# Attention into a mixture of experts: key maxima, one-hots, halves of w1 and four clears dealt anew to the attention's steps

## The chip, the core and the metric

The kernel runs on one core of one Trainium2 chip. A core has engines that each work through their own instructions in order: TensorE (PE in the rows) multiplies matrices into PSUM; VectorE (DVE), ScalarE (ACT) and GpSimd (POOL) work on elements; SyncE (SP) issues DMA transfers. They wait for each other through semaphores. The metric is the device time of one execution in microseconds, lower is better. Times before are the median of three runs.

## What is computed

First attention over 4 batches, 8 heads, 768 positions of width 64, with keys of a local window of 16 to either side and with one summary key and value for every block of 32 positions (the maximum of the block's keys, the mean of its values). The result, 3072 rows of 512 numbers, goes through a mixture of 8 experts, of which each row uses the two with the largest noisy gate:

```python
k_sum = k.reshape(B, H, nb, block, D).max(axis=3)
v_sum = v.reshape(B, H, nb, block, D).mean(axis=3)
...
a = np.exp(scores_all)
a = a / (np.sum(a, axis=-1, keepdims=True) + 1e-09)
...
top2 = np.argpartition(-noisy_logits, 2, axis=1)[:, :2]
...
h = np.maximum(x[mask] @ w1[e], 0.0)
out[mask] += top2_w[mask, k, None] * (h @ w2[e])
```

`out` starts as zeros. In the kernel that is done by eight DMA writes of zeros ("clears"), 384 rows or 768 KB each, after which the experts add their rows by gather and scatter.

## The kernel before

The attention works on 24 tiles of 128 rows, six to a batch. A loop over steps t is software-pipelined: in step t TensorE makes the scores of tile t + 2 (`mask_sums`, L316, and `scores`, L326), multiplies tile t's weights with its values (`av`, L365), transposes tile t + 1's weights (`p_trans`, L348) and tile t - 1's result (`x_pe`, L419). VectorE takes the row maxima of the scores (`smax`, L336 and L337: `nm`, which ScalarE's exponentials L342 need) and normalizes tile t (`norm`, L396 to L400). GpSimd lays out the keys of tile t + 3 (`kx`, L126, L131) and splits the result into two halves of float16 (L406, L411), which SyncE stores to `xd` (`x_out`, L414). SyncE also loads the queries four steps ahead (`load_q`, L118) and the values two steps ahead (`v_load`, L296 and L297). Step 9 begins on TensorE at 56.38 us, step 10 at 62.59, step 11 at 70.53, step 13 at 78.01, step 16 at 95.81, step 17 at 100.95, step 18 at 105.74 and step 21 at 118.42.

Everything else in the attention is hung into the steps by a table: `at(time, f, ...)` puts a call at a step number with a fraction, and the fraction says where in the step's code `run` or `vector_work` takes it. So t + 0.02 stands right behind the step's store of `x`, t + 0.1 behind VectorE's normalization of the step, t + 0.9 at its end. What hangs there and is touched by the change:

- `k_piece` (L232, tile `kmax`): the maxima over blocks of the keys of one pair of heads; four for each batch, in `KP`. `load_k` (L112, tile `kb`) loads the keys of two pairs of heads, at the times in `KL`. Batch b's keys lie in buffer b % 2.
- `gate_lh`, `gate_o`, `gate_f` (L592, L624, L631): for a group of four tiles, one-hots of a row's place (`lh`, `oc`) and their product with the row's values (`rh`); `gate_t` (L643) multiplies them on TensorE one step later, and `gate_u` (L647) adds that to the table `acc`, from which the experts' row numbers are decoded (`decode`, L654 to L660) in step 19. `make_table` holds the steps of a group.
- `w_load` (L716 for w1, L719 for w2; tile `stg`, four buffers), and `w_part`: the first expert's w1 comes in four pieces of 512 KB, each split in halves into a high float16 part (ScalarE, L737) and the rest (VectorE, L735, tile `w1l`). The four loads of w2 at 17.9, 18.9, 21.9 and 22.9 take the same four buffers, so each waits for the halves that read the piece before it.
- `x_gather` (L94) and `x_trans` (L862): in steps 20 and 21 GpSimd gathers three chunks of 128 of the first expert's rows from `xd`, and SyncE transposes them by DMA into `xte`. Right after the attention TensorE multiplies these with w1 (`mm1_pe`, L884).
- `clear` (L1101): one write of zeros to 384 rows of the output, from a tile of zeros. `XG[3]` is a gather buffer that is cleared at the very start and first gathered into after the attention.

After the attention the first expert's products begin with 384 columns, while the last tables are made; then come the other seven experts, in which TensorE is fed from prefetched weights and gathered rows.

Of the kernel before, what the change touches and what calls it, by code (L numbers as in the profile page):

```python
# [8 lines left out]
F32 = mybir.dt.float32  # L9
# [53 lines left out]
def attn_moe(ctx, tc, qt, kt, vt, wgn, noise, w1, w2, out):  # L63
# [150 lines left out]
    XG = []  # L214
# [198 lines left out]
    def x_out(t):  # L413
        xd_w.append(nc.sync.dma_start(xd[t * P:(t + 1) * P], XR[t]))  # L414
# [221 lines left out]
    def gate_t(b, o, hs=(0,), i=1):  # L636
        tb = o[:, i, GO:GO + 3 * NS]
        n = 2 * GN * len(hs)
        for h in hs:
            lh, rh, _ = GR[b, h]  # L640
            for j in range(2 * GN):
                n -= 1
                nc.tensor.matmul(tb, lh[:, j], rh[:, j], start=(h == hs[0] and j == 0), stop=(n == 0),  # L643
                                 skip_group_check=True)

    def gate_u(b, o, i=1):
        nc.vector.tensor_add(ACC, ACC, o[:, i, GO:GO + 3 * NS].rearrange("p (v c) -> p v c", v=3))  # L647
# [44 lines left out]
    def w_alloc(e):  # L692
        w1_alloc(e)
        w2_alloc(e)
# [398 lines left out]
    def at(t, f, *a):  # L1093
        todo.setdefault(round(t, 3), []).append((f, a))
# [3 lines left out]
    def clear(zero, n):  # L1098
        a = cleared[0]
        cleared[0] += n  # L1100
        nc.sync.dma_start(out[a * P:(a + n) * P].rearrange("(c p) d -> p c d", p=P),  # L1101
                          zero[:, None, :].to_broadcast([P, n, DM]))
# [15 lines left out]
    at(0.2, v_sums_out, 0)  # L1118

    w_alloc(0)  # L1120
    for i, (l, h, z) in enumerate(((6, 8, 9), (7, 9, 10), (15, 19, 20), (16, 20, 21))):
        at(l, w_load, 0, i)
        for k in range(2):
            at(h + 0.9, w_part, i, k, 0)
            at(z + 0.1, w_part, i, k, 1)
    VS = [4, 10, 15]
    KP = ((1, 1, 2, 2), (5, 6, 7, 8), (10, 12, 13, 14))
    KL = ((-1, 0), (3, 5), (9, 10))
    VL = [(1, 2), (6, 7), (12, 13)]
    for b in range(B - 1):  # L1130
        for h in range(HP):
            at(KP[b][h] + 0.1, k_piece, b + 1, h)
            if h % 2 == 0:
                at(KL[b][h // 2], load_k, b + 1, h, 2)
        for i in range(2):
# [6 lines left out]
    for i in range(3):  # L1142
        at(4.9 + 2 * i, fill, i)
    at(20.8, last_init)
    for g in range(5):
        u = 4 * g + 6
        at(u - 0.7, gate_gt, g)
        at(u - 0.65, gate_gc, g)
        at(u + 0.3, gate_gl, g)
        at(u + 0.35, gate_gd, g)  # L1150
# [22 lines left out]
    def make_table(b, v, lh, oc, rh):  # L1173
        at(v + 0.8, gate_v, b, False)
        at(lh + 0.1, gate_lh, b)
        at(oc + 0.1, gate_o, b)
        at(rh + 0.1, gate_f, b)
        at(rh + 1.28, lambda b, t: gate_t(b, PO[t], (0,)), b, rh + 1)
        at(rh + 1.4, lambda b, t: gate_u(b, PO[t]), b, rh + 1)

    make_table(0, 10, 11, 11, 13)
    make_table(1, 13, 14, 15, 15)
    make_table(2, 16, 17, 17, 18)
    at(19.1, decode, TB0, 0, 3)
    at(22.6, gate_a, 4)
    at(22.8, gate_v, 3, False)

# [24 lines left out]
    for t in range(-2, NT - 1):  # L1212
        u = t + 3
# [103 lines left out]
    gate_p(4)  # L1317
    spair.close()
    banks.append(ctx.enter_context(tc.tile_pool(name="banks", bufs=4, space=PSUM, reuse_waits="tile")))
    for i in range(4):  # L1320
        clear(PREV[2], 3)
    x_out(NT - 1)
    for i in range(4):
        clear(PREV[2], 3)
    w_load(1, 0, "sh0")
    w_load(1, 2, "sl0")
# [259 lines left out]
```

## Time and profile before

| | |
|---|---|
| median of three runs | 649.4 us (647.72 to 653.26) |
| profiled execution, its own time | 649.54 us |
| its span in the trace | 647.7 us |
| TensorE busy | 625.7 us, 97% of the span |
| VectorE busy | 478.5 us, 74% |
| GpSimd busy | 349.9 us, 54% |
| ScalarE busy | 306.3 us, 47% |

The span is the stretch between the first and the last recorded instruction; 1.8 us of the execution lie outside. A busy share says how long an engine worked, not whether others waited for it; for that one looks in the engine's order of time at the idle stretch before an instruction and at what released it. In the rows below, the time in brackets is that idle stretch.

### The profile page before, as it was taken

What the parts mean: (1) busy time and instruction counts of PE and PEld (TensorE: products, weight loads), DVE (VectorE), ACT (ScalarE), POOL (GpSimd) and SP (SyncE); (2) the same over time, 40 slices, a digit from 0 to 9 for tenths busy, and PEclk for the clock granted to TensorE, in tenths of its full rate; (3) what the DMA queues carried; (4) which work ended last, traced back from release to release, by engine and by line L of the source; (5) the groups of instructions that cost most, each with busy time, mean ns of one, the idle gap of its engine ahead of it and who ended that gap; (6) DMA issues with size and microseconds to landing.
All of it is one profiled execution on the core that took longest, in us unless ns stands there. A gap on an engine that the chain in (4) does not pass through costs nothing.

```text
span 647.7 us, 14116 instructions
## 1 busy us (share of the span) xinstructions
PE 625.7 (97%) x5407; PEld 368.3 (57%) x5407; DVE 478.5 (74%) x897; ACT 306.3 (47%) x647; POOL 349.9 (54%) x531
## 2 busy tenths in 40 slices
PE   8998899899999999999999999999999999999996
PEld 7777678765545544554465446545554555455543
DVE  7858898886786879577947886787778677956511
ACT  3788787851533552265235424541564165325300
POOL 5675777735635757653655465555546451632042
PEclk9999999999999999999999999999999999999999
DMA  8999998899978686456835572667266723431031
GB/s 302 321 331 376 300 356 280 197 339 312 274 162 181 212 181 184 157 194 159 210 134 167 164 237 102 196 162 232 97 182 160 236 72 110 149 127 50 2 100 52
DMA packets 104568, 125.63 MB, mean 194 GB/s; under 512 B 58393, under 2 KB 59681, under 8 KB 104492
## 3 DMA queue, kind: packets, MB, share of 16 engines
q1 hardware_dynamic: 92348, 88.37, 46.4%
q0 software_dynamic: 12144, 36.28, 17.9%
q8 instruction: 44, 0.72, 0.5%
q14 instruction: 32, 0.26, 0.1%
HBM read 87.38 MB, written 26.21 MB: 175 GB/s over the span
## 4 chain that ended last, share of the span: by engine, by line
PE 76%; issue 8%; DMA 6%; DVE 4%; POOL 2%; ACT 1%; POOLq 1%; SPq 0%; another core or an unknown queue 0%; ACTq 0%; DVEq 0%
PE pt L1039 33%; PE h L920 23%; DMA q<-in_qt_dram 5%; PE h L884 4%; PE a L920 4%; PE pt L1036 3%; PE o L365 2%; PE s L326 2%; PE pt L348 2%; DMA kb<-in_kt_dram 1%; POOL prev L94 1%; PE pt L419 1%; DVE s L336 1%; POOL out_dram L94 1%; PE pt L439 1%
## 5 line engine op out<-in xcount | busy, mean ns | idle before, releaser
L94 POOL DMA_INDIRECT out_dram<-y,tb x48 | 64.5, 1345 | 153.4 <-DVE y L1062 140.7
L1039 PEld LDWEIGHTS <-hth 128*128 128x128 f16 x768 | 74.9, 98 | 89.1
L1039 PE MATMUL pt<-w2h,htl 128*128 128x512 f16 x376 | 88.8, 379 | 0.0
L1039 PE MATMUL pt<-w2h,hth 128*128 128x512 f16 x376 | 88.8, 379 | 0.0
L1039 PE MATMUL pt<-w2l,hth 128*128 128x512 f16 x376 | 88.8, 379 | 0.0
L94 POOL DMA_INDIRECT xg<-xd,tb x53 | 70.2, 1324 | 32.4 <-DVE oc L659 17.1
L920 PE MATMUL h<-tx,sh 128*128 128x402 f16 x336 | 77.8, 333 | 0.0
L1062 DVE SCALAR_TENSOR_TENSOR y<-pt,tb,prev 128x512 f32<-128x512 f32 x42 | 31.5, 749 | 52.4 <-PE pt L1039 48.0
L742 DVE SCALAR_TENSOR_TENSOR w2l<-stg,w2h 128x1024 f16<-128x1024 f32 x32 | 49.1, 1542 | 27.8 <-ACT w2h L725 26.4
L342 ACT ACTIVATE p<-s,nm 128x120 f32<-128x120 f32 x188 | 53.0, 389 | 23.0 <-DVE nm L337 20.1
L1039 PEld LDWEIGHTS <-htl 128*128 128x128 f16 x384 | 37.6, 98 | 45.3
L920 PEld LDWEIGHTS <-w1h 128*128 128x128 f16 x448 | 43.1, 98 | 33.0 <-issue 1.4
L94 POOL DMA_INDIRECT prev<-out_dram,tb x42 | 51.9, 1237 | 13.6 <-issue 13.6
L789 POOL TENSOR_TENSOR t<-xte 128x804 f32<-128x804 f16 x24 | 38.9, 1646 | 36.6 <-DVE t L745 31.1
L920 PE MATMUL h<-xte,w1h 128*128 128x402 f16 x224 | 56.3, 333 | 0.0
L942 ACT ACTIVATE p<-h 128x402 f32<-128x402 f32 x28 | 14.2, 506 | 74.0 <-issue 65.4
L817 ACT ACTIVATE tx<-t 128x804 f16<-128x804 f32 x28 | 23.7, 869 | 50.4 <-DVE t L745 50.4
L920 PEld LDWEIGHTS <-sh 128*128 128x128 f16 x336 | 32.6, 97 | 24.9
L920 PE MATMUL h<-tx,sl 128*128 128x402 f16 x168 | 42.2, 332 | 0.0
L336 DVE TENSOR_REDUCE s<-s 128x4 f32<-128x480 f32 x47 | 30.9, 658 | 12.0 <-PE s L326 10.6
L928 DVE SCALAR_TENSOR_TENSOR htl<-h,hth 128x402 f16<-128x402 f32 x56 | 31.9, 569 | 8.4 <-ACT hth L925 8.3
L770 ACT ACTIVATE sh<-ws 128x1536 f16<-128x1536 f32 x14 | 20.8, 1483 | 36.6 <-DVE ws L745 32.5
(240 smaller groups left out, 1232.6 us busy)
## 6 DMA issues: line engine op xcount, KB each, us to landing
stg<-in_w_dram SPq DMA_DIRECT2D x62, 512.0 KB
q<-in_qt_dram SPq DMA_DIRECT2D x24, 256.0 KB
hth<-in_vt_dram SPq DMA_DIRECT2D x8, 768.0 KB
xd<-xr SPq DMA_DIRECT2D x24, 256.0 KB
out_dram<-prev SPq DMA_DIRECT2D x8, 768.0 KB
kb<-in_kt_dram SPq DMA_DIRECT2D x6, 768.0 KB
htl<-in_vt_dram SPq DMA_DIRECT2D x12, 260.0 KB
vw<-in_vt_dram SPq DMA_DIRECT2D x12, 260.0 KB
```

Source lines behind the costliest of these rows:

```text
L94: return nc.gpsimd.indirect_dma_start(**kw)
L336: nc.vector.tensor_reduce(m, SC[t, a], axis=AX.X, op=OP.max)
L342: nc.scalar.activation(PE_[t, a][:, hp, :], SC[t, a][:, hp, :], AF.Exp, bias=NM[t][:, a, hp:hp + 1], scale=SCALE)
L742: nc.vector.scalar_tensor_tensor(lo, SG[e, i], sc, hi, op0=OP.mult, op1=OP.subtract)
L770: nc.scalar.activation(h, x, AF.Copy, scale=W1S)
L789: nc.gpsimd.tensor_tensor(tt(e, 0 if low else j), xb(e, *i, low), xb(e, *o, low), op=OP.subtract)
L817: nc.scalar.activation(TX[e][:, 0, j - 1], t_of(e, j), AF.Copy)
L884: nc.tensor.matmul(ph[:, :n], w[wn][:, c, f * P:(f + 1) * P], x[:, xo + c, c0:c1], start=(k == 0), stop=(k == 11), skip_group_check=hook i ...
L920: nc.tensor.matmul(o, lhs[a][:, c], rhs[b][:, c], start=start and n == 0, stop=stop and n == 5, skip_group_check=True)
L928: nc.vector.scalar_tensor_tensor(HT[1][:, f, c0:c1], c, 0.0, HT[0][:, f, c0:c1], op0=OP.max, op1=OP.subtract)
L1039: nc.tensor.matmul(py, hx[:, f, c * P:c * P + P], w[:, f, :], start=first, stop=final, skip_group_check=True)
L1062: nc.vector.scalar_tensor_tensor(y, py[:, :d], gw, pv[:, :d], op0=OP.mult, op1=OP.add)
```

## The change

Four of the eight clears move from behind the attention to the beginnings of steps 18 to 21 and write zeros from `XG[3]`; the other four stay. The first piece of w1 is loaded in step 7 instead of 6 and the second in step 11 instead of 7; the halves of all four pieces are dealt to steps one by one, and the low halves are entered into the table after the one-hots, so that they stand behind these in the same step. Two of the key maxima of batch 2 (`KP[1]`) go from steps 5 and 6 to step 4; one of batch 3 (`KP[2]`) goes from step 12 to 10, and the second load of its keys to the front of step 10. The first two tables are made one step later in part.

```diff
     w_alloc(0)
-    for i, (l, h, z) in enumerate(((6, 8, 9), (7, 9, 10), (15, 19, 20), (16, 20, 21))):
+    lows = []
+    for i, (l, h, z) in enumerate(((7, (9, 13), (10, 17)), (11, (14, 16), (17, 18)), (15, (17, 18), (19, 21)),
+                                   (16, (19, 20), (21, 21)))):
         at(l, w_load, 0, i)
         for k in range(2):
-            at(h + 0.9, w_part, i, k, 0)
-            at(z + 0.1, w_part, i, k, 1)
+            at(h[k] + 0.9, w_part, i, k, 0)
+            lows.append((z[k] + 0.1, i, k))
     VS = [4, 10, 15]
-    KP = ((1, 1, 2, 2), (5, 6, 7, 8), (10, 12, 13, 14))
-    KL = ((-1, 0), (3, 5), (9, 10))
+    KP = ((1, 1, 2, 2), (4, 4, 7, 8), (10, 10, 13, 14))
+    KL = ((-1, 0), (3, 5), (9, 10.02))
...
     at(20.8, last_init)
+    for t in range(18, 22):
+        at(t + 0.02, clear, XG[3].bitcast(F32), 3)
...
-    make_table(0, 10, 11, 11, 13)
-    make_table(1, 13, 14, 15, 15)
+    make_table(0, 10, 12, 13, 14)
+    make_table(1, 13, 15, 15, 16)
     make_table(2, 16, 17, 17, 18)
     at(19.1, decode, TB0, 0, 3)
+    for u, i, k in lows:
+        at(u, w_part, i, k, 1)
...
-    for i in range(4):
+    for i in range(2):
         clear(PREV[2], 3)
     x_out(NT - 1)
-    for i in range(4):
+    for i in range(2):
         clear(PREV[2], 3)
```

Three places in the order of the instructions. The first is VectorE from the end of step 4's normalization to step 5's; `s` is a bank of scores, `nm` its negated row maxima. Before:

```order
L400 TENSOR_TENSOR x<-o,ri 128x512
L336 TENSOR_REDUCE s_916<-s_916 128x4
L337 TENSOR_SCALAR nm<-s_916 128x4
L336 TENSOR_REDUCE s_913<-s_913 128x4
L337 TENSOR_SCALAR nm<-s_913 128x4
L396 TENSOR_SCALAR r<-o 128x8
L398 RECIPROCAL ri<-r 128x8
L400 TENSOR_TENSOR x<-o,ri 128x512
L232 TENSOR_REDUCE kmax<-kb_92 128x24
```

The same place in the changed kernel:

```order
L400 TENSOR_TENSOR x<-o,ri 128x512
L232 TENSOR_REDUCE kmax<-kb_92 128x24 x2
L336 TENSOR_REDUCE s_919<-s_919 128x4
L337 TENSOR_SCALAR nm<-s_919 128x4
L336 TENSOR_REDUCE s_916<-s_916 128x4
L337 TENSOR_SCALAR nm<-s_916 128x4
L396 TENSOR_SCALAR r<-o 128x8
L398 RECIPROCAL ri<-r 128x8
L400 TENSOR_TENSOR x<-o,ri 128x512
```

Two maxima that stood behind the normalizations of steps 5 and 6 now stand ahead of step 5's score reductions.

The second is VectorE from the end of step 9 to the beginning of step 11. Before:

```order
L560 TENSOR_TENSOR mc_163<-mc_162,mt 128x8
L735 SCALAR_TENSOR_TENSOR w1l_308<-stg,w1h_307 128x512 x2
L336 TENSOR_REDUCE s_1469<-s_1469 128x4
L337 TENSOR_SCALAR nm<-s_1469 128x4
L336 TENSOR_REDUCE s_1466<-s_1466 128x4
L337 TENSOR_SCALAR nm<-s_1466 128x4
L396 TENSOR_SCALAR r<-o 128x8
L398 RECIPROCAL ri<-r 128x8
L400 TENSOR_TENSOR x<-o,ri 128x512
L735 SCALAR_TENSOR_TENSOR w1l_308<-stg,w1h_307 128x512 x2
L232 TENSOR_REDUCE kmax<-kb_93 128x24
L569 RECIPROCAL wa<-wden 128x4
```

In the changed kernel:

```order
L560 TENSOR_TENSOR mc_163<-mc_162,mt 128x8
L336 TENSOR_REDUCE s_1463<-s_1463 128x4
L337 TENSOR_SCALAR nm<-s_1463 128x4
L336 TENSOR_REDUCE s_1460<-s_1460 128x4
L337 TENSOR_SCALAR nm<-s_1460 128x4
L396 TENSOR_SCALAR r<-o 128x8
L398 RECIPROCAL ri<-r 128x8
L400 TENSOR_TENSOR x<-o,ri 128x512
L232 TENSOR_REDUCE kmax<-kb_93 128x24 x2
L735 SCALAR_TENSOR_TENSOR w1l_308<-stg,w1h_307 128x512
L569 RECIPROCAL wa<-wden 128x4
```

Four halves of w1l ahead of the maximum are gone from here, two maxima stand together, and one half follows them.

The third is SyncE's queue from step 19 to step 21 (`vw` are values, `xd` the store of x, `xte` the transposes, the last row of the piece before is the third load of w2). Before:

```order
L297 DMA vw<-in_vt_dram 32x2x520
L414 DMA xd<-xr 128x1024
L296 DMA vw<-in_vt_dram 64x2x520
L297 DMA vw<-in_vt_dram 32x2x520
L414 DMA xd<-xr 128x1024
L862 DMA_TRANSPOSE xte<-xg_157 128x8x128
L862 DMA_TRANSPOSE xte<-xg_158 128x8x128
L862 DMA_TRANSPOSE xte<-xg_159 128x8x128
L719 DMA stg<-in_w_dram 128x2x512
```

In the changed kernel:

```order
L1101 DMA out_dram<-xg_160 128x3x512
L296 DMA vw<-in_vt_dram 64x2x520
L297 DMA vw<-in_vt_dram 32x2x520
L414 DMA xd<-xr 128x1024
L1101 DMA out_dram<-xg_160 128x3x512
L296 DMA vw<-in_vt_dram 64x2x520
L297 DMA vw<-in_vt_dram 32x2x520
L414 DMA xd<-xr 128x1024
L1101 DMA out_dram<-xg_160 128x3x512
L862 DMA_TRANSPOSE xte<-xg_157 128x8x128
L862 DMA_TRANSPOSE xte<-xg_158 128x8x128
L862 DMA_TRANSPOSE xte<-xg_159 128x8x128
```

A clear of 768 KB stands behind every store of x, the last one right ahead of the three transposes. The first of the four, in step 18, stands above this piece.

## Rows read from the trace of the kernel before

**Rows 1.** The page of the profile: its first line.
```profile
span 647.7 us, 14116 instructions
```

**Rows 2.** Busy time by step: window, its us, each engine's busy us, granted clock, DMA.
```profile
core 0: us, PE busy (x) PEld busy (x) DVE busy (x) ACT busy (x) POOL busy (x), PEclk, DMA share, GB/s
...
78.01:84.59 6.58, 5.29 (x120) 4.49 (x119) 6.46 (x24) 5.66 (x19) 4.43 (x8) 1.00 1.06 373
...
100.95:105.74 4.79, 4.79 (x114) 4.18 (x113) 4.37 (x14) 4.39 (x14) 3.39 (x12) 1.00 1.01 368
...
105.74:110.59 4.85, 4.39 (x82) 3.51 (x82) 3.52 (x10) 3.73 (x13) 4.69 (x7) 1.00 0.57 178
...
118.42:125.99 7.57, 5.22 (x113) 4.20 (x113) 6.84 (x31) 5.74 (x17) 6.04 (x11) 1.00 0.93 227
...
130.46:168.20 37.74, 36.52 (x265) 20.99 (x263) 28.02 (x94) 13.29 (x25) 18.14 (x33) 1.00 0.95 319
...
168.20:600.00 431.80, 431.80 (x2499) 228.14 (x2499) 333.15 (x450) 189.12 (x306) 229.89 (x300) 1.00 0.58 164
...
39.38:130.46 91.08, 81.41 (x1747) 69.57 (x1747) 76.53 (x258) 75.35 (x236) 63.89 (x113) 1.00 0.95 302
```

**Rows 3.** TensorE in order of time: start us, us, instruction, [idle before, who ended it].
```profile
57.09 1.05 PE L326 MATMUL s<-kx,q 64*64 64x120 f32 x32 [0.36 <-DMA q<-in_qt_dram]
...
63.26 1.05 PE L326 MATMUL s<-kx,q 64*64 64x120 f32 x32 [0.31 <-DMA q<-in_qt_dram]
...
79.45 0.35 PE L316 MATMUL s<-mask,identb 64*64 64x384 bf16 x2 [1.08 <-ACT p L342]
...
98.85 0.18 PE L515 MATMUL o<-m,tri 128*128 128x32 f16 x1 [0.78 <-DVE m L501]
...
121.27 1.15 PE L365 MATMUL o<-vw,pts 120*64 120x65 f32 x32 [1.40 <-ACT p L342]
...
125.40 0.66 PE L419 MATMUL pt<-ident,x 128*128 128x128 f32 x4 [0.95 <-ACT lt L446]
```

**Rows 4.** VectorE in order of time, same columns: steps 5 and 10.
```profile
40.71 0.67 DVE L336 TENSOR_REDUCE s<-s 128x4 f32<-128x480 f32 x1 [3.41 <-PE s L326]
...
71.10 0.95 DVE L232 TENSOR_REDUCE kmax<-kb 128x24 f32<-128x768 f32 x1 [2.69 <-DMA kb<-in_kt_dram]
```

**Rows 5.** SyncE's DMA issues in order of time: start us, us to issue, transfer.
```profile
33.38 1.12 SPq L112 DMA_DIRECT2D kb<-in_kt_dram  x1
...
63.19 0.38 SPq L112 DMA_DIRECT2D kb<-in_kt_dram  x1
...
107.59 0.33 SPq L414 DMA_DIRECT2D xd<-xr  x1
...
120.96 5.71 SPq L862 DMA_TRANSPOSE xte<-xg  x3
```

**Rows 6.** VectorE by line, 20 to 130 us: count | busy us, mean ns | idle.
```profile
L232 DVE TENSOR_REDUCE kmax<-kb 128x24 f32<-128x768 f32 x12 | 11.2, 944 | 2.7 <-DMA kb<-in_kt_dram 2.7
...
L735 DVE SCALAR_TENSOR_TENSOR w1l<-stg,w1h 128x512 f16<-128x512 f32 x8 | 5.6, 734 | 0.0
...
L631 DVE TENSOR_TENSOR rh<-oc,val 128x1344 f16<-128x1344 f16 x3 | 3.6, 1197 | 0.1
```

**Rows 7.** DMA by window: window, its us, granted clock, DMA share, GB/s.
```profile
core 0: us, , PEclk, DMA share, GB/s
...
106.00:108.00 2.00, 1.00 0.19 55
...
124.00:129.00 5.00, 1.00 1.12 185
...
136.00:152.00 16.00, 1.00 1.03 377
```

**Rows 8.** TensorE in order of time: first expert's products, first and second half.
```profile
130.46 0.81 PE L884 MATMUL s<-xte,w1h 128*128 128x384 f16 x4
...
168.20 0.87 PE L884 MATMUL h<-xte,w1h 128*128 128x420 f16 x4 [1.13 <-ACT xte L871]
```

## The prediction

> **What bounds the kernel now.** I read the stage windows first, then TensorE's order of time for its gaps, then VectorE, SyncE's queue and the DMA windows, to see who ends each gap. The profiled execution took 649.54 us; its span is 647.7 us [rows 1], so 1.8 us lie outside the span. The median of the runs shown is 649.4 us, 0.1 us less, so I work against 649.5.
>
> In the table by steps [rows 2] the reader is to see two halves. From 168.20 to 600 us TensorE (PE) is busy 431.80 of 431.80 us, at a granted clock of 1.00 (the higher of its two levels): nothing in that half can be won or lost unless it is starved, and the change touches nothing that runs there. The change acts only between step 4 and about 168 us. From step 5 to 130.46 us PE is busy 81.41 of 91.08 us, so 9.7 us are idle; from 130.46 to 168.20 it is 36.52 of 37.74, 1.2 us idle. Together 10.9 us, 1.7% of the time, is the most that any rearrangement can win.
>
> Who ends those gaps [rows 3]: in steps 9 and 10 (57.09 and 63.26) loads of q, 0.36 and 0.31 us; in step 13 (79.45) ScalarE (ACT) exponentials, 1.08 us; in step 16 (98.85) VectorE's m, 0.78 us; in step 21 ACT, 1.40 us (121.27) and 0.95 us (125.40). The ACT waits of steps 13 and 21 are VectorE's (DVE's) one step back, since the exponentials wait for nm, which DVE makes after all it was given in the step before. In step 13 DVE is busy 6.46 of 6.58 us while PE is busy 5.29 [rows 2]. That stretch starts late, at 71.10, where DVE had waited 2.69 us for the keys that the maximum reads [rows 4]; the load of these was issued at 63.19 [rows 5], 7.9 us earlier.
>
> **The change, part by part.** No instruction of any weight is added or taken away; work moves between steps, and four of eight clears go from the stretch after the attention into steps 18 to 21.
>
> *First w1 loads later (step 6 to 7, step 7 to 11).* From step 6 to the key load at 63.19, 512 KB less stand in SyncE's queue. At the rate of a full queue, 377 GB/s [rows 7], 512 KB take 1.4 us, more than either q wait. I take both as gone: 0.7 us. Bounds: nothing, and 0.7.
>
> *Key maxima.* Batch 3: the second goes from step 12 to step 10, right behind the first, on the same load; steps 9 and 10 lose three w1 halves ahead of that wait, and one stands behind it. The keys land about 1.4 us earlier (69.7), two maxima of 0.94 us and one half of about 0.7 [rows 6] follow, and DVE is at 72.3 where it now is at 72.05: no gain at the start of the stretch, but the steps behind are lighter by one maximum, and step 11 by two one-hots (lh moves to 12, oc to 13). The 1.08 us of step 13 go. The m of step 15 no longer has rh (1.20 us [rows 6]) ahead of it, because rh goes to step 16: I take half of the 0.78 us. Sum: 1.5 us won, bounds 0 and 1.9 (both waits whole).
>
> Batch 2: both first maxima go to step 4. Their load is issued at 33.38 [rows 5]. By the 7.9 us that the other key load took it lands at 41.3; DVE, which now stands idle for 3.41 us until 40.71 [rows 4], would then stand at the maxima and start step 5's reductions 1.9 us behind them, at 43.2, 2.5 us late. Queued behind are nm, the exponentials, and on ACT the copies that free TensorE's next PSUM banks. Step 5 loses its own maximum (0.94 us) on DVE, so DVE catches up, but PE keeps what it lost. If the load lands by 38.8, nothing is late. Between 0 and 2.5 I take 1.2 us lost, since the queue is shorter at 33 us than at 63. The two q waits above vanish in either case.
>
> *Halves of w1l dealt anew.* Steps 17 and 18 now hold two and one of them, and the table's sum moves to 17. Step 17: DVE 4.37 us + 2 x 0.7 = 5.8 us, where the step lasts 4.79 with PE full [rows 2]; 1.0 us lost. Step 18: 3.52 + 0.7 = 4.2 of 4.85, hidden. Bounds 0 and 2 (if step 19 loses as much). Step 20 loses both of its halves, 1.4 us ahead of step 21's nm; of the 1.40 and 0.95 us in step 21 I take 1.2 as won (bounds 0.5 and 2.3). Three halves at the end of step 21 stand before step 22's row ranks, whose users are later; nothing.
>
> Up to the first expert's products, then: 0.7 + 1.5 + 1.2 won, 1.2 + 1.0 lost, 1.2 us net. TensorE reaches them at about 129.3 instead of 130.46 [rows 8].
>
> *The clears.* Each is 768 KB; behind each other they and the loads around them ran at 377 GB/s, 2.1 us each [rows 7]. They seem to fit: DMA runs at 55 GB/s from 106 to 108. But they stand ahead of the three transposes that make the first expert's tokens (xte), on one queue. Those are issued from 120.96 [rows 5], and PE needs the third at 130.46; from 124 to 129 DMA share is 1.12 at only 185 GB/s [rows 7], which I read as the transposes, so they have hardly a microsecond to spare now. What goes through the engines after the change, from the w2 load of step 17 on: two w2 loads (1.0 MB), two of q (0.5), four pairs of v (1.6), four stores of x (1.0), four clears (3.1) and three gathers (0.8), 8.1 MB; at 377 GB/s 21.6 us. The first can't start before DVE has made step 17's w1l, because that load takes the buffer: about where the store of x goes out now, 107.59 [rows 5], less 1.2, plus 1 us until bytes move: 107.4. So the queue reaches the transposes at 129.0. Each costs SyncE 1.9 us to issue (5.71 / 3 [rows 5]); on the engines I take 1 us, as between 0.7 (256 KB at 377 GB/s) and 1.4 (at 185). All three have landed at 132.0. PE waits 2.7 us, and its products begin 1.5 us later than now. Bounds: landed by 129.3, no wait; landed at 136, 6.7 us of waiting (gathers that crawl beside a full queue, transposes at 1.9 us each).
>
> That SyncE's transfers are served one behind the other is what the key load shows: 7.9 us for 768 KB, in a stretch where a full queue moves that in 2.1. The Trainium skill, DMA: Bandwidth & Descriptors, section "Queues, rings and completion order", says that SyncE owns one ring on each DMA engine and that an engine takes its descriptors in ring order. By that rule the transposes can't pass the clears, and the sum is the one above; if they could, it would be the first rival's. The trace agrees with the rule as far as it shows it; no row has a clear ahead of a transpose.
>
> *After 130.* Half of the clears no longer follow the attention, so 3.1 MB, 8.3 us of queue, less stands before the gathers of the first expert's remaining tokens. PE's 1.13 us at 168.20 [rows 8] is a wait for a copy of such tokens. Since it names ACT and no DMA, I take half: 0.5 us won, bounds 0 and 1.1. A scatter must wait until the clears have landed; they land earlier.
>
> Sum: 649.5 + 1.5 - 0.5 = 650.5 us.
>
> **The rivals.**
> 1. *The clears hide.* The transposes pass them or still land in time. For: 55 GB/s at 106 to 108. Against: the queue model above. Then the 1.2 us net stay, and 0.5 to 1.1 behind them: 649.5 - 1.2 - 0.8 = 647.5.
> 2. *Clears starve the transposes* (slower). One mechanism: transposes and gathers behind 3.1 MB of clears land at 136 instead of 132. PE then starts 5.5 us late and wins 0.5 back: 654.5. It decides as soon as the third transpose lands after 131.
> 3. *Nothing that is moved matters.* Waits are handed on to fetches and to other engines, the steps last as long as now, transposes land at 130.5: 649.5.
> 4. *The keys' wait is worth more.* The 2.69 us at 71.10 go whole, steps 11 to 16 run at PE's pace, and step 4 costs nothing: 0.7 + 2.7 + 1.9 + 1.2 = 6.5 won, 1.0 lost, clears hidden, 0.8 behind: 643.2.
>
> **How the numbers follow.** Forecast 0.42; rival 1 0.28; rival 2 0.12; rival 3 0.11; rival 4 0.07. The likeliest time is 650.5. The forecast's own spread is about 649 to 652.5 (landing of the transposes 1.5 us either way). A range from 646 to 654 holds the forecast, rivals 1 and 3 whole, and leaves out rival 4 and most of rival 2. One per cent, about what a measurement of this kernel can tell from no change, is 6.5 us: faster than 643 asks for nearly all of rival 4, 0.04; slower than 656 for rival 2 at its worst, 0.07; within 0.89.
>
> **What would show it.** In the changed profile: no q wait at steps 9 and 10; DVE idle before two maxima in step 4, ended by a key load; no ACT wait in step 13; step 17 longer by about a microsecond; four clears on SyncE before the transposes; and TensorE's first product of line 884 with an idle of about 2.7 us before it, ended by a DMA. If that wait is absent, rival 1 is right and I was wrong about the queue; if it is above 5 us, rival 2. The windows behind 170 us must be as full as before; if they are not, the whole reading is wrong.

## The result and the profile after

| | before | changed |
|---|---|---|
| median | 649.47 us (6 runs, 647.72 to 653.26) | 659.58 us (6 runs, 655.21 to 659.95) |
| profiled execution | 649.54 us | 659.86 us |
| ratio to before | 1 | 1.0136, 95% interval 1.0107 to 1.0165 |

The changed kernel is 1.4% slower, some 9 us. The forecast was 650.5 us, with a range from 646 to 654. The two profiled executions lie 10.3 us apart, and the table of windows shows where. First the page's first line and the windows of the changed kernel (window, its us, each engine's busy us, granted clock, DMA share, GB/s); its steps 5, 12, 13, 17, 18, 19, 20 and 21 begin at 40.52, 73.62, 80.64, 100.93, 106.68, 112.68, 118.39 and 122.04.

```profile
span 658.0 us, 14111 instructions
...
core 0: us, PE busy (x) PEld busy (x) DVE busy (x) ACT busy (x) POOL busy (x), PEclk, DMA share, GB/s
...
73.62:80.64 7.02, 4.54 (x81) 3.85 (x80) 5.85 (x30) 5.45 (x17) 6.77 (x13) 1.00 1.05 277
...
100.93:106.68 5.75, 5.69 (x122) 4.71 (x122) 5.61 (x19) 5.33 (x17) 4.05 (x12) 1.00 0.91 260
106.68:112.68 6.00, 3.98 (x83) 3.32 (x82) 5.86 (x12) 4.25 (x14) 5.84 (x8) 1.00 0.40 132
112.68:118.39 5.71, 5.71 (x91) 5.10 (x90) 4.13 (x10) 4.57 (x15) 4.04 (x6) 0.70 1.03 353
...
138.90:142.00 3.10, 3.10 (x11) 1.80 (x12) 0.00 (x0) 0.00 (x0) 0.00 (x0) 0.50 0.92 330
...
138.90:178.50 39.60, 38.92 (x263) 21.97 (x264) 26.16 (x87) 12.28 (x23) 15.03 (x24) 0.94 0.73 241
178.50:610.30 431.80, 431.80 (x2498) 227.96 (x2498) 331.94 (x449) 188.95 (x306) 230.84 (x298) 1.00 0.57 164
```

Two windows of the kernel before that [rows 2] lacks, its steps 12 and 19:

```profile
74.17:78.01 3.84, 3.84 (x81) 3.44 (x80) 3.82 (x17) 2.39 (x7) 3.76 (x6) 1.00 1.00 343
110.59:114.78 4.19, 4.19 (x91) 3.78 (x90) 3.48 (x9) 4.06 (x14) 3.85 (x7) 1.00 0.85 269
```

From the second half of the first expert's products on (178.50, before 168.20) both kernels take the same 479.5 us to the end of the span, at full clock. All of the 10.3 us are older:

| stretch | before, us | changed, us | difference |
|---|---|---|---|
| start to step 5 | 39.38 | 40.52 | +1.1 |
| steps 5 to 11 | 34.79 | 33.10 | -1.7 |
| step 12 | 3.84 | 7.02 | +3.2 |
| steps 13 to 16 | 22.94 | 20.29 | -2.7 |
| steps 17, 18, 19 | 4.79, 4.85, 4.19 | 5.75, 6.00, 5.71 | +1.0, +1.2, +1.5 |
| steps 20 to the end of the attention | 15.68 | 15.79 | +0.1 |
| wait ahead of line 884 | 0 | 4.72 | +4.7 |
| first to second half of the products | 37.74 | 39.60 | +1.9 |

The first line is no work of the change: over the profiled executions of this study step 5 began between 38.3 and 40.7 us, changed code or not. TensorE's order of time in the changed kernel names who ended each gap (start us, us, instruction, [idle before, releaser]):

```profile
74.92 0.35 PE L316 MATMUL s<-mask,identb 64*64 64x384 bf16 x2 [0.95 <-DVE ri L398]
...
78.11 1.15 PE L365 MATMUL o<-htl,pts 120*64 120x65 f32 x30 [1.53 <-DMA htl<-htl]
...
103.53 0.75 PE L643 MATMUL o<-rh,lh 128*128 128x168 f16 x8
...
112.09 0.66 PE L419 MATMUL pt<-ident,x 128*128 128x128 f32 x4 [2.02 <-ACT lg L455]
...
112.87 1.58 PE L326 MATMUL s<-kx,q 64*64 64x120 f32 x32
...
118.57 0.99 PE L326 MATMUL s<-kx,q 64*64 64x120 f32 x32
...
124.87 1.15 PE L365 MATMUL o<-vw,pts 120*64 120x65 f32 x32 [1.27 <-ACT p L342]
...
138.90 1.44 PE L884 MATMUL s<-xte,w1h 128*128 128x384 f16 x4 [4.72 <-DMA xte<-xg]
```

The largest gap is the one that the forecast put there: 4.72 us of waiting for the transposes. Behind it the granted clock is 0.50, the lower of its two levels, until 142 us; the first products take 1.44 us where they took 0.81 [rows 8]. Without the waits ahead of the second half (0.59 and, in [rows 8], 1.13) the products last 39.0 instead of 36.6 us; that these 2.4 us are the clock's is what e7 shows below. The same happens in small at 112 us: 2.02 us idle, and then line 326 takes 1.58 instead of 0.99.

SyncE's queue of the changed kernel, in order of time (start us, us to issue, transfer), and under it the three transposes by themselves (shortest, median and longest issue in ns, first and last start) and the second one alone:

```profile
67.13 0.38 SPq L112 DMA_DIRECT2D kb<-in_kt_dram  x1
68.92 0.88 SPq L288 DMA_DIRECT2D htl<-htl  x1
...
109.05 0.38 SPq L719 DMA_DIRECT2D stg<-in_w_dram  x1
...
126.18 0.39 SPq L1101 DMA_DIRECT2D out_dram<-xg  x1
127.61 9.04 SPq L862 DMA_TRANSPOSE xte<-xg  x3
```

```profile
L862 SPq DMA_TRANSPOSE xte<-xg x3: 2064/2064/4723, 127.6 to 134.6; - x3
```

```profile
129.77 4.72 SPq L862 DMA_TRANSPOSE xte<-xg  x1
```

The transposes now take 9.04 us to issue, not 5.71 [rows 5]: 2.06, 4.72 and 2.06. The second, begun at 129.77, holds SyncE, which comes to the third only at 134.6 us. Before the change, the same spread of the sums of values stood ahead of the second key load:

```profile
69.48 0.88 SPq L288 DMA_DIRECT2D htl<-htl  x1
70.47 1.49 SPq L112 DMA_DIRECT2D kb<-in_kt_dram  x1
```

### The profile page after: what moved, and what is told of

Same layout as the page of the kernel before. It is cut to its first block, busy times and chain, and to the rows that moved or that the text cites. A ratio compares the mean times of both kernels' runs of the same rounds, so it can differ in the third digit from the quotient of the medians.

```text
span 658.0 us, 14111 instructions
## 1 busy us (share of the span) xinstructions
PE 630.8 (96%) x5407; PEld 371.2 (56%) x5407; DVE 480.1 (73%) x897; ACT 306.6 (47%) x647; POOL 351.7 (53%) x531
## 4 chain that ended last, share of the span: by engine, by line
PE 76%; issue 8%; DMA 6%; DVE 4%; POOL 3%; SPq 1%; ACT 1%; POOLq 1%; ACTq 0%
PE pt L1039 32%; PE h L920 23%; PE h L884 4%; DMA vw<-in_vt_dram 4%; PE a L920 4%; PE pt L1036 3%; PE o L365 2%; PE s L326 1%; DMA htl<-htl 1%; PE pt L348 1%; PE o L248 1%; POOL prev L94 1%; SPq L862 1%; DVE s L336 1%; PE h L1039 1%
## 5 line engine op out<-in xcount | busy, mean ns | idle before, releaser
L789 POOL TENSOR_TENSOR t<-xte 128x804 f32<-128x804 f16 x24 | 38.9, 1646 | 36.6 <-DVE t L745 31.4
```

What stands on the lines that cost most here:

```text
L789: nc.gpsimd.tensor_tensor(tt(e, 0 if low else j), xb(e, *i, low), xb(e, *o, low), op=OP.subtract)
```

## The experiments

Each ratio is that of a kernel to the kernel before, run on the same chip in the same hours, with its 95% interval; 0.1% is 0.65 us. The result above and the groups e1 to e4, e5 to e8, e9 to e12, e13 to e16, and e17 with e18 come from different chips or hours, so a difference of two ratios carries both intervals. "Early clears" are the four in steps 18 to 21, "w1" the loads and halves dealt anew.

**e1, the changed kernel with all clears behind the attention.**

```diff
-    for t in range(18, 22):
-        at(t + 0.02, clear, XG[3].bitcast(F32), 3)
...
-    for i in range(2):
+    for i in range(4):
         clear(PREV[2], 3)
     x_out(NT - 1)
-    for i in range(2):
+    for i in range(4):
         clear(PREV[2], 3)
```

> The changed kernel with one part undone: all eight clears stand behind the attention again; the rest of the change stays. Theory Q (queue): the 4.72 us that TensorE waits before the first expert's products come from the clears ahead of the transposes in SyncE's queue, and the low clock right behind that wait (granted clock 0.50 from 138.9 to 142 us) is its consequence; without the clears that wait shrinks to under 1 us and the time falls by about 6.6 us, to about 653, and what stays is the 3.7 us by which TensorE ends the attention late. Theory G (gathers): the transposes are late because the table of the first expert is decoded 3.7 us later and the gathers behind it; then the wait stays at 3 us or more and the time is 657 or above.

1.0030 (1.0004 to 1.0056), median 649.7. The early clears are 1.06% of the changed kernel's 1.36% (give or take 0.4), about 6.9 us. TensorE's wait for the transposes, in the profile:

```profile
132.46 0.81 PE L884 MATMUL s<-xte,w1h 128*128 128x384 f16 x4 [0.89 <-DMA xte<-xg]
```

It is 0.89 us, and the products run at 0.81 us from the first. Theory G, that the gathers are late by the table, falls: VectorE still ends the decoding 1.6 us later than in the kernel before, counted from step 5, and the wait is small all the same.

**e2, the kernel before with the early clears alone.** The same lines the other way round.

> The kernel before with one part of the change alone: four of the eight clears in steps 18 to 21, nothing else. Theory Q: 3.1 MB more stand ahead of the transposes, the third lands at about 134 to 136, TensorE waits 3 to 5 us at line 884 and loses another 1 to 2 us by the lower clock behind that wait: 654 to 656, and the steps up to 17 start as in the kernel before. Theory G: the gathers are as early as before, the wait is at most 1.5 us and the time is 649 to 651.

1.0051 (1.0025 to 1.0078), median 651.6. The profiled execution, 655.0 us and so at the upper end of its twelve runs (648.9 to 655.5), has the whole picture:

```profile
134.48 1.44 PE L884 MATMUL s<-xte,w1h 128*128 128x384 f16 x4 [3.97 <-DMA xte<-xg]
```

```profile
134.48:138.00 3.52, 3.52 (x13) 2.19 (x14) 0.00 (x0) 0.00 (x0) 0.15 (x1) 0.50 1.01 356
```

A wait of 3.97 us, then 3.5 us at a granted clock of 0.50. The steps up to 21 begin within 0.5 us of the kernel before from step 11 on, as expected. The median is below what was expected, half of the 1.06% of e1.

**e3, the changed kernel with w1 as before; e4, the kernel before with w1 alone.**

```diff
-    for i, (l, h, z) in enumerate(((6, 8, 9), (7, 9, 10), (15, 19, 20), (16, 20, 21))):
+    for i, (l, h, z) in enumerate(((7, (9, 13), (10, 17)), (11, (14, 16), (17, 18)), (15, (17, 18), (19, 21)),
+                                   (16, (19, 20), (21, 21)))):
...
```

> The changed kernel with the loads of w1 and the dealing of its halves put back; clears, key maxima and tables stay. Theory Q: steps 17 to 19 lose their halves of w1l and the idle of 2.0 us with its low clock at 110 to 118 us; TensorE ends the attention 3 to 4 us sooner, but the clears still stand ahead of the transposes, so the wait grows to 5 us or more and the time is 655 to 658: little is won. Theory G: the table is decoded earlier, the wait goes with it, and the time is 650 to 652.

> The kernel before with only the w1 part of the change: later loads and halves dealt anew. Theory Q: steps 17 to 19 last longer by 3 to 4 us together (two halves of w1l in step 17 hold back the score maxima, and the load of w2 behind them holds SyncE's queue to about 109 us); no wait for the transposes beyond 1 us; 652 to 654. Theory G: the transposes come late by the table, a wait of 3 us or more shows at line 884, 655 or above.

The fence is the first part of e4's edit; e3 undoes the same. e3: 1.0124 (1.0087 to 1.0161); putting w1 back wins nothing that can be told from 1.0136. Its wait at line 884 is 2.41 us in the profile, not the 5 or more that theory Q expected, with a granted clock of 0.57 behind it (134.66 to 138); that profiled execution, 653.7 us, is among the fastest of its six (653.5 to 659.8). e4: 1.0004 (0.9974 to 1.0035); alone it costs nothing. Its profile has no wait for q, as forecast, and a gap of 1.11 us in step 18, with no loss of clock behind it. Expected for e4 were 652 to 654: what w1 wins in steps 5 to 11 (32.96 us instead of 34.79) it mostly gives back in step 18 and in a wait of 1.08 us ahead of line 884.

**e5, the changed kernel with the second key load back at the end of step 10; e8, the kernel before with that line alone.**

```diff
-    KL = ((-1, 0), (3, 5), (9, 10.02))
+    KL = ((-1, 0), (3, 5), (9, 10))
```

> The changed kernel with one line undone: the second load of batch 3's keys stands at the end of step 10 again, behind the spreading of the sums of values (htl<-htl, line 288), instead of ahead of it. Theory S (spread): in the changed kernel that load of 768 KB delays the spread; TensorE waits 1.53 us for it at 78.11 and step 12 lasts 7.0 us instead of 3.8. With the load back, the wait for htl is gone, step 12 lasts 4 us or less, and the time falls by about 3 us, to about 656.5; the wait ahead of line 884 stays at 4 to 5 us. Rival D (VectorE): step 12 is long because the maxima stand together in step 10; then it stays at 6 us or more and the time at 659.

> The kernel before with one line of the change alone: the second load of batch 3's keys at the front of step 10, ahead of the spread htl<-htl. Theory S: TensorE waits 1.5 to 2.5 us for htl in step 12 and the time is 650.5 to 651.5, 2 to 3 us above the kernel before. Rival D: without the maxima put together, the spread lands in time, no wait for htl, 648 to 649.

Theory S was right about the place; its time isn't borne out. In e8 the wait is there:

```profile
79.83 1.15 PE L365 MATMUL o<-htl,pts 120*64 120x65 f32 x30 [2.83 <-DMA htl<-htl]
```

Step 12 takes 7.7 us instead of 3.8; yet e8 is 1.0016 (0.9991 to 1.0041), not told from no change. The profiled execution, 652.5 us, lies at the upper end of its twelve (647.7 to 653.6), and whether the others have the wait isn't known. And e5, where step 12 is down to 4.7 us, is 1.0157 (1.0135 to 1.0179), no faster than the changed kernel. Its profile shows what stands behind:

```profile
80.47 0.69 PE L365 MATMUL o<-htl,pts 120*64 120x65 f32 x17 [1.74 <-issue]
...
94.18 0.84 PE L266 MATMUL pt<-hth 128*24 128x130 f32 x18 [2.30 <-issue]
```

Two waits of 1.74 and 2.30 us that nothing in the profile explains ("issue") take the place of the one removed. Counted from step 6, e5 is 3.0 us ahead of the changed kernel at the start of step 13 and 0.4 us behind it at step 17: the time won does not reach step 17.

**e6, the changed kernel with both undone (key load back, clears late).**

> The changed kernel without its two suspected losses: the second key load at the end of step 10, and all eight clears behind the attention; w1, key maxima and tables as changed. Theory: the two losses are separate and add up, about 3 us and 7 to 9 us of the changed kernel's time, so this one takes 646 to 647.5, 1 to 2 us under the kernel before. Rival: what is left of the change loses on its own in steps 17 to 19; then 649 or more.

1.0035 (1.0013 to 1.0056): as e1. The rival came out: the two losses do not add up, since the key load shows none here, in e5 or in e8 (whose interval leaves room for 2.6 us), and what is left of the change loses about 2 us by itself.

**e7, matmuls that fill the wait.**

```diff
+    keep_on = s_bank(1)
+    for i in range(80):
+        nc.tensor.matmul(keep_on[:, 0:P], identb, identb, start=True, stop=True, skip_group_check=True)
-    mm1_pe(0, 0, 0, s_bank(1), {2 * DC: lambda: x_pe(NT - 1)})
+    mm1_pe(0, 0, 0, keep_on, {2 * DC: lambda: x_pe(NT - 1)})
```

> The changed kernel with 80 matmuls of 128 columns put in front of the first expert's products, into the bank that these overwrite: TensorE works through most of its wait of 4.7 us instead of standing idle (the 90 of the start took 7.92 us, so at the full clock 80 should take 4 to 7). Theory: behind the wait the granted clock was 0.50 for 3.1 us and 0.77 for 4 us, since TensorE had stood idle; with the filler the first products start no more than 1 to 2 us later, run at a granted clock of 1.00, first to second half takes 37 us or less instead of 39.6, and the time is 657 to 660. Rival: the products are slow for their operands or by the DMA beside them, then first to second half stays near 39.6 whatever stands ahead, and the time rises by what the filler overshoots.

TensorE's order of time, and the window behind the filler:

```profile
133.96 4.63 PE L1294 MATMUL s<-identb 128*128 128x128 bf16 x80
138.48 0.81 PE L884 MATMUL s<-xte,w1h 128*128 128x384 f16 x4
...
179.00 1.56 PE L884 MATMUL h<-xte,w1h 128*128 128x420 f16 x4 [3.91 <-ACT xte L871]
```

```profile
138.48:142.00 3.52, 3.52 (x38) 2.33 (x40) 0.41 (x1) 1.53 (x3) 0.15 (x1) 1.00 0.97 346
```

The products start at 138.48 with no idle time, take 0.81 us, and the granted clock is 1.00. From first to second half it is 36.6 us without the wait at the end (40.52 less 3.91): the 2.4 us are the clock's. The rival, operands or the DMA beside the products, isn't needed: the operands are the same, and the DMA moves 346 GB/s here and 330 in the changed kernel's slow stretch. The Trainium skill, TensorE: Matmul & The Clock Gate, Part 1, says that TensorE's clock is halved after it has stood idle and comes back while it works; the runs agree, with 0.50 behind 4.72 us of idle time and 1.00 behind 4.63 us of filler. The total, 1.0132 (1.0104 to 1.0159), doesn't show the 2.4 us: in the profile they come back as the wait of 3.91 us for the second half's tokens, behind which the granted clock is 0.50 again from 179 to 182 us. From there to the end this execution, the slowest of its six, takes 482.0 us instead of 479.5.

**e9, two of the early clears behind the transposes.**

```diff
-    for t in range(18, 22):
-        at(t + 0.02, clear, XG[3].bitcast(F32), 3)
+    for t in (18.02, 19.02, 21.9, 21.9):
+        at(t, clear, XG[3].bitcast(F32), 3)
```

> The changed kernel with two of its four early clears, those of steps 20 and 21, put right behind the third transpose in SyncE's queue; as many bytes are written in the same stretch, only the order differs. Theory Q: 1.5 MB less ahead of the transposes is 4.2 us of queue, so the third lands by 135 instead of 138.6, the wait ahead of line 884 falls from 4.7 to 1.5 us or less, the clock stays at 1.00, and the time falls by 5 us or more, to about 654. Rival B (bandwidth): it is the traffic of the clears beside gathers and transposes, wherever they stand; then the wait stays at 3 us or more and the time within 2 us of the changed kernel.

1.0105 (1.0069 to 1.0142), median 654.9. The wait is 1.92 us, the clock behind it still falls (0.61 from 138 to 142 us), and a new gap of 0.90 us appears among the products, for ACT's lt at line 446. Of the 5 us that were expected the ratio shows 0.3%, which the two intervals don't tell from nothing; the profiled execution, 658.35 us, is the slowest of its six.

**e10, the tables alone; e11, the steps of the key maxima alone.**

```diff
-    make_table(0, 10, 11, 11, 13)
-    make_table(1, 13, 14, 15, 15)
+    make_table(0, 10, 12, 13, 14)
+    make_table(1, 13, 15, 15, 16)
```

```diff
-    KP = ((1, 1, 2, 2), (5, 6, 7, 8), (10, 12, 13, 14))
+    KP = ((1, 1, 2, 2), (4, 4, 7, 8), (10, 10, 13, 14))
```

> The kernel before with the first two tables alone made later in part, as in the change. Theory T (tables cost): the products rh of 1.2 us and the one-hots of step 15 and 16 come into fuller steps, steps 15 to 18 last 1 to 2 us longer, 649.5 to 651. Rival: they fill VectorE's idle time, no step changes by over 0.5 us, 648 to 649.

> The kernel before with the four steps of the key maxima alone changed (two in step 4, two in step 10); both key loads as before. By the prediction's sum: step 13 loses its wait of 1.08 us for the exponentials, step 4 to 5 gains about 1.2 us of waiting for the keys, the time is 648 to 650. Rival M (maxima cost more): in step 10 the second maximum holds back the score maxima of the next step by 0.9 us on top of the wait for the keys, and step 5 the same by up to 2.5 us; 650.5 or more.

e10: 1.0006 (0.9984 to 1.0028). e11: 1.0021 (0.9996 to 1.0047). Neither can be told from no change. But they bear on a step of the forecast: e11 keeps step 13's wait,

```profile
78.74 0.35 PE L316 MATMUL s<-mask,identb 64*64 64x384 bf16 x2 [1.08 <-ACT p L342]
```

and so do e4 (1.18 us) and e12 (1.08), while in e10 it is gone. So the key maximum doesn't lift it. In the kernel before, the two one-hots (lines 592 and 624, together 1.6 us from 75.84 on) stand on VectorE right ahead of the score maxima for which ScalarE waits 1.72 us until 78.28; that moving them lifts the wait is likely, though e17 below, with neither, lacks it too in its one profile.

**e12, w1 alone with one half less in step 17** (`(10, 17)` becomes `(10, 14)`).

> The kernel before with the w1 part of the change, but with the second low half of the first piece in step 14 instead of 17. With it in step 17, VectorE held two halves there, step 18 waited 1.11 us and the load of w2 that needs that buffer stood in SyncE's queue to 105.5 us. If these two halves are what costs steps 17 to 19 their gain, the wait in step 18 falls under 0.5 us and the time is 646 to 647, 1 to 2 us under the kernel before; if step 14 has no room for a half either, the gain is lost there and the time is 648 to 649.

1.0013 (0.9991 to 1.0036). The wait in step 18 is gone, but 1.08 us at step 16 (VectorE's m) and 1.18 us of "issue" at 106.89 are there: no gain.

**e13, the changed kernel with the same half in step 14.**

> The changed kernel with the second low half of w1's first piece in step 14 instead of 17. In the changed kernel the load of w2 that takes this piece's buffer stood at the head of SyncE's queue until 109.05 us, and the clears behind it. Theory L (late start): that is what makes the early clears dearer here than in the kernel before; with the half in step 14 the load goes out by 104 to 106, the transposes land 2 to 4 us sooner, the wait ahead of line 884 is under 3 us and the time 654 to 656. Rival: the start of the queue does not matter, wait over 4 us, 658 or more.

1.0148 (1.0114 to 1.0182). Theory L falls. The load of w2 goes out early, as it was to, and the next in the queue waits instead:

```profile
101.39 0.38 SPq L719 DMA_DIRECT2D stg<-in_w_dram  x1
...
109.14 0.33 SPq L414 DMA_DIRECT2D xd<-xr  x1
```

The store of x holds SyncE to 109.14 us, and the first clear follows at 109.51; the wait at line 884 is 5.03 us.

**e14, early clears and w1; e15, early clears and tables; e16, the changed kernel with the tables back.** Their edits are those above, joined.

> The kernel before with the early clears and the w1 part, nothing else. Theory L: the two meet in SyncE's queue, which starts late behind the load of w2; the wait is 4 us or more and the time 1% over the kernel before (about 654.5), twice what the clears cost alone (0.5%), although w1 alone costs nothing. Rival: no meeting, the two add: 0.5 to 0.6%, about 651.5.

> The kernel before with the early clears and the later tables, nothing else. If the tables, made later, push the decoding and the gathers behind, and thereby the transposes deeper into the clears, the wait is above 4.5 us and the time 1% over the kernel before (about 654.5). Theory L expects no such meeting: 0.5 to 0.6%, about 651.5.

> The changed kernel with the first two tables made as before. If the tables are what makes the clears dearer: 655 to 656. Theory L: the halves of w1 and SyncE's late start are left in, so little changes, 658 to 660, wait ahead of line 884 at 4 to 5 us.

e14: 1.0145 (1.0112 to 1.0177): these two parts alone make the whole loss, although w1 alone costs 0.0004. e15: 1.0087 (1.0057 to 1.0118), with a wait of 3.03 us at line 884; its interval overlaps that of the clears alone (e2). e16: 1.0139 (1.0094 to 1.0185), with a wait of 4.07: taking the tables back wins nothing. In e14's profile TensorE ends the attention 0.9 us sooner than in e2 (it began step 5 1.1 us sooner), and the products begin at the same time:

```profile
134.67 1.44 PE L884 MATMUL s<-xte,w1h 128*128 128x384 f16 x4 [5.01 <-DMA xte<-xg]
```

So a head start ahead of the transposes turns into waiting for them. That tells why w1's gain is lost, not why the pair costs 1% more than the clears alone.

**e17 and e18, all four early clears behind the third transpose, without and with w1.**

```diff
+    for t in (21.9, 21.9, 21.9, 21.9):
+        at(t, clear, XG[3].bitcast(F32), 3)
...
```

> The kernel before with the four early clears right behind the third transpose in SyncE's queue (step 21) and nothing else: as early as they can be without standing ahead of it. Theory Q: no clear is ahead of the transposes, the wait ahead of line 884 is 1 us or less, the granted clock behind it stays 1.00, and the time is that of the kernel before within 0.2%. Rival B (bandwidth of the clears beside gathers and transposes, or their stores in the way of what follows): 0.4% or more above the kernel before, as with the clears in steps 18 to 21.

> The kernel before with the w1 part and the four early clears right behind the third transpose. With the clears in steps 18 to 21 and the w1 part it was 1.45% above the kernel before. Theory Q: all of that is the order in SyncE's queue; with the clears behind the transposes the wait of 5.0 us ahead of line 884 falls to about 1 us (1.08 with w1 alone) and the time is within 0.3% of the kernel before. If the two parts meet in another place, for instance behind 160 us where the second half's tokens are gathered, 0.7% or more is left.

e17: 1.0102 (1.0066 to 1.0137), median 655.2. e18: 1.0127 (1.0087 to 1.0166), median 657.2. In e17 the wait at line 884 is 0.15 us, as theory Q said, in e18 2.02, not about 1, and the time is lost all the same, at another place. SyncE's queue, ScalarE and TensorE of e17, each in order of time:

```profile
125.65 5.08 SPq L1101 DMA_DIRECT2D out_dram<-xg  x4
130.83 1.27 SPq L414 DMA_DIRECT2D xd<-xr  x1
```

```profile
138.63 0.63 ACT L408 ACTIVATE xr<-x 128x512 f16<-128x512 f32 x1 [7.13 <-DMA xd<-xr]
139.16 0.26 ACT L446 ACTIVATE lt<-pt 128x128 f32<-128x128 f32 x1
```

```profile
139.48 0.47 PE L450 MATMUL pt<-ident,lt 128*128 128x128 f32 x1 [6.09 <-ACT lt L446]
```

The stores of x now stand behind the clears. The last tile's xr, which ScalarE writes, needs the buffer that such a store reads; ScalarE waits 7.13 us, lt is queued behind that copy, and TensorE stands idle for 6.09 us between its products, with a granted clock of 0.50 behind it until 143 us. In e18 it is 6.54 us at 143.13. So it is the order in the queue, but not ahead of the transposes alone: whatever follows the four clears is late. That is the second half of rival B, the clears in the way of what follows, and its number came too. Its first half, the traffic itself, isn't needed for the 6 us; that it has no part at all wasn't tried.

None of these kernels beats the kernel before; nearest are e4 and e10.

## Why the prediction was wrong

The path that it named was right: the clears stand ahead of the transposes, and TensorE waits for these. What failed are the price of VectorE's halves of w1l behind step 17, the start of SyncE's queue, the time of a transpose, the reading of step 21's wait, and the clock, for which it had no term. Worked from its own terms, against the profiled execution:

- *Up to step 17.* 1.0 us won was the sum (0.7 of q, 1.5 at steps 13 and 16, 1.2 lost at step 5); TensorE reaches step 17 1.2 us sooner, seen from step 5, but some 0.6 of it is work that moved on into step 17 (see there). So the sum came out by luck, the way only partly. The q waits are gone, and w1 is what takes them away (e4); but step 9 is only 0.2 us shorter, and in step 10 TensorE waits 0.44 us for GpSimd's kx where it waited for q. Steps 5 to 11 are 1.7 us shorter since two waits that the forecast left alone are not there, 0.77 us for exponentials in step 8 and 0.98 without a releaser in step 10. Step 5's reductions begin at 42.51 us where it was 40.71 [rows 4]; 1.1 of that is the later start, so 0.7 us was lost where 1.2 was forecast (VectorE's rows below). The late start hides part of the loss: in e16, with the same maxima, step 5 begins at 38.69 us and lasts 5.90 where the kernel before took 4.67, with 1.03 us of waiting for ScalarE's lt. The 1.08 us of step 13 were given to a lighter VectorE, by a maximum and two one-hots; the maximum doesn't bring them (e11). And the second key load, moved to the front of step 10, got no price at all, though it was moved past the spread of the sums in SyncE's queue: step 12 is 3.2 us longer, 2.3 of it by this load (e5), and 0.95 is a wait for VectorE's ri. Steps 13 to 16 are 2.7 us shorter.
- *Steps 17 to 19.* Step 17 was forecast 1.0 us longer and is 0.96 longer, but that is luck: the forecast put it down to VectorE, and TensorE is busy 5.69 of the 5.75 us. It does 0.75 us more of its own work, line 643's product of the second table, which stood in step 16 before. VectorE's two halves come only behind it, at 107.37, in TensorE's step 18. That step was called hidden; here the sum failed. A half of w1l was costed at 0.7 us, and the two took 2.56 together (last section); the score maxima behind them made ScalarE wait 1.75 us and TensorE 2.02, and then the clock was low. Steps 18 and 19: 2.7 us.

```profile
40.78 1.81 DVE L232 TENSOR_REDUCE kmax<-kb 128x24 f32<-128x768 f32 x2 [1.78 <-DMA kb<-in_kt_dram]
42.51 0.66 DVE L336 TENSOR_REDUCE s<-s 128x4 f32<-128x480 f32 x1
```

```profile
110.81 1.11 ACT L342 ACTIVATE p<-s,nm 128x120 f32<-128x120 f32 x4 [1.75 <-DVE nm L337]
```

The first fence is VectorE in step 4 of the changed kernel, the second ScalarE in step 18.

- *Step 21.* 1.2 us won were forecast, none came in the sum. The 0.95 us for lt are gone, 0.66 for values come new at 132.20, and 1.27 us of waiting for the exponentials stand where 1.40 stood. The forecast read this wait as VectorE's one step back. But the exponentials that end it start in both kernels right behind ScalarE's own copies, with no idle time, and 2.4 us (changed: 1.7) after their nm was made, at 117.7 and 121.9 us. So in the kernel before a lighter VectorE had nothing to win there.

```profile
119.12 1.08 ACT L351 ACTIVATE pts<-pt 120x512 f32<-120x512 f32 x2 [0.50 <-PE pt L419]
120.09 1.12 ACT L342 ACTIVATE p<-s,nm 128x120 f32<-128x120 f32 x4
```

```profile
123.66 1.12 ACT L342 ACTIVATE p<-s,nm 128x120 f32<-128x120 f32 x4
```

The first fence is ScalarE before, the second in the changed kernel.

- *The clears.* The mechanism was the forecast's. The third transpose was expected at 132.0, and TensorE could start at 138.9. Two terms were too small. The queue started at 109.05, not about 106.4, since the load of w2 stands there until step 17's w1l is made, and that was late. And a transpose was given 1 us on the engines. By the windows below (columns as in the first table), some 8.0 MB have moved from 109.05 to 132.33 us (an estimate from us and GB/s), about the 8.1 that the forecast put ahead of the transposes: at 132.3, not 129.0. From there to TensorE's start are 6.6 us for three, by this estimate 2.2 each. The wait is 4.72 us instead of 2.7, near the 5 us above which the forecast named the second rival. (It also let that rival decide once the third transpose lands after 131, which its own 132.0 does.) The measured 659.6 is beyond that rival's 654.5 because the attention ended late too, and by the clock.

```profile
109.05:127.61 18.56, 15.22 (x287) 13.07 (x287) 15.85 (x55) 14.12 (x45) 14.82 (x23) 0.91 0.95 333
127.61:132.33 4.72, 3.88 (x64) 3.39 (x63) 4.64 (x12) 4.45 (x14) 3.16 (x3) 1.00 1.31 385
132.33:138.90 6.57, 1.66 (x37) 1.34 (x37) 5.40 (x17) 1.47 (x5) 4.64 (x12) 0.86 1.15 158
```

- *The clock.* No term for it: 2.4 us behind the wait (e7), and part of step 19.
- *After 130.* Half of the 1.13 us was forecast as won; 0.59 is left of it. The number came out; its reason isn't shown, since with the same early clears this wait is 2.09 us in e14 and nothing in e2.

From 650.5: 2.7 at steps 18 and 19, 1.3 at step 21, 2.0 of wait, 2.4 of clock and 1.1 of a later start make 660.0, less 0.2 won up to step 17: 659.8, where 659.9 was measured. The trace tells it so for one execution; the runs tell that 6.9 of the 9 us go with the early clears and about 2 with the rest, no part of which costs by itself what these runs could tell.

Open stays why the clears cost 0.5% alone and 1.45% together with w1: moving w1's half (e13) and the clears (e18) did not separate it. The profiled execution of e2 has a wait nearly as long as the changed kernel's, and half of its runs lie 4 us or more below that; no profile shows one of those. So the clears alone may cost some 6 us in one execution and little in another. The 2.4 us by which e14's profiled execution is longer than e2's are nearly all its wait of 2.09 us ahead of the second half. Open are also these waits, 0.6 to 3.9 us in some kernels, with and without early clears, and none in others, and which part of the tables makes e15 dearer than e2, if it is.

## What to carry to other kernels

A transfer that nobody waits for is not free on a queue that somebody waits for: 3 MB of clears ahead of the transposes cost 3.3 us alone (e2) and 6.9 in the changed kernel (e1), and moved behind them, ahead of the stores whose buffers ScalarE needed, 6.6 us (e17). List, for a moved transfer, everything issued behind it on its queue up to where the queue next runs dry, and who waits for each; then allow, behind any TensorE wait of some microseconds, for a stretch at the lower clock. It doesn't follow every such wait: behind 2.36 us at 77.58 in e1 the clock stayed at 1.00, behind 1.55 us at 75.39 in e13 it was 0.50. A wait removed upstream of such a queue can come back as a longer wait there, as w1's gain did in e14.

## What the runs showed of the hardware that was not expected

A VectorE instruction of one shape has no fixed price. The halves of w1l took 0.73 us in the mean before [rows 6] and 0.97 in the changed kernel over the same stretch (seven of the eight; the last, at 130.2, took 1.65). The two of step 17 took 2.56 us, the first alone 1.65, while GpSimd was at work throughout, with line 411's subtraction from 107.28 on and then a copy of keys. That copy was slow too, 1.87 us for two where it takes 0.95 at 115.83. The group of line 735 (count | busy us, mean ns), then VectorE and GpSimd in order of time:

```profile
L735 DVE SCALAR_TENSOR_TENSOR w1l<-stg,w1h 128x512 f16<-128x512 f32 x7 | 6.6, 973 | 0.0
```

```profile
107.37 2.56 DVE L735 SCALAR_TENSOR_TENSOR w1l<-stg,w1h 128x512 f16<-128x512 f32 x2
```

```profile
108.42 1.87 POOL L126 COPY kx<-kb 128x384 f32<-128x384 f32 x2
...
115.83 0.95 POOL L126 COPY kx<-kb 128x384 f32<-128x384 f32 x2
```

That the two hinder each other is read from this overlap; it wasn't tried apart. The other thing: TensorE has waits with no releaser at the same lines in most of these kernels (266, 326 and 365 in steps 13 to 18), up to 2.3 us long. In e5 they are longer where another wait ahead of them was removed; that the one brings the other isn't shown.
